# A gated recurrence and a routed feed-forward on one core: TensorE in program order, expert blocks over all turns, two weight buffers

## The chip, the cores and the metric

The kernel runs on one core of a Trainium2 chip. The core has a matrix engine (TensorE, PE in the profile; its weight loads are PEld), VectorE (DVE), ScalarE (ACT), GpSimd (POOL), and a sync engine (SP) that issues DMAs; GpSimd issues the indirect ones. Each engine works through its own queue in order and waits on semaphores for the others. The metric is the device time of one execution in microseconds; lower is better.

## The reference

Two parts, all in float32. First a recurrence over time, for 4 batches, 8 heads, 768 steps and head width 48:

```python
f = 1.0 / (1.0 + np.exp(-f_logit))
for t in range(S):
    state = f[:, :, t, :, None] * state + np.einsum('bhd,bhe->bhde', k[:, :, t], v[:, :, t])
    y[:, :, t] = np.einsum('bhd,bhde->bhe', q[:, :, t], state)
```

Then y, as 3072 rows of 384, goes through a feed-forward of 8 experts, two for each row:

```python
noisy_logits = x @ w_gate + np.log1p(np.exp(x @ w_noise)) * noise
top2 = np.argpartition(-noisy_logits, 2, axis=1)[:, :2]
# top2_w: softmax over the two chosen logits
for e in range(E):
    for k in range(2):
        mask = top2[:, k] == e
        h = np.maximum(x[mask] @ w1[e], 0.0)
        out[mask] += top2_w[mask, k, None] * (h @ w2[e])
```

w1 of an expert is 384 x 1024, w2 1024 x 384: 1.5 MB each.

## The kernel before

**The recurrence** is done in six chunks of 128 steps. `chunk(c, b)` handles one chunk of one batch, all eight heads. Inside a chunk the sum over earlier steps is built in seven levels (steps within pairs, fours, eights, up to 128), so that a chunk is a fixed list of matmuls: transposes of f, q and k (L208), the diagonal (`diag`, L231), for each level 16 score matmuls (`sc`, L247), then y from the scores A and v (L268) plus, from the second chunk on, y from the carried state (L272), and transposes and products for the next state (`kp` L281, `xp` L286, `ds` L295). Between two levels, the scores of the level are copied under a mask into A (copy_predicated on VectorE, L253), qP is multiplied by the decay T (VectorE, L257), and kQ and T are multiplied on GpSimd (L259, L261). The next level's `sc` reads qP and kQ, so a level cannot begin before these are done. The last chunk needs no next state and leaves out `kp` and `ds`.

**Routing.** `route(c)` follows the four batches of a chunk: logits (`lg`, L316), noise, the two best experts of each row, and a running place of each row in its expert's list (`rk`, L354, the last matmuls of the routing). Eight indirect DMAs from GpSimd then write row numbers into a table in DRAM, `ids` (L369, one for each batch and choice), and four DMAs write the rows with their gates to `xd` (L349). `choose(c)` picks from the filled lists LIST[c] blocks of 128 rows of one expert each (0, 9, 8, 8, 8 and 22: 55 in all), and writes where in `ids` each begins (`row_no`) and whether its weights must be loaded (`load_no`): the load is skipped if the block that used the same weight buffer last, NW blocks back, had the same expert.

**A block.** `fetch` issues the loads of a block, on SP: the block's row numbers from `ids` into `places` (L441), two weight loads into one of NW buffers each (L446), and on GpSimd the gather of rows from `xd` into `rows_in` (L447; three buffers). `block` then does: transposes (`bx`, L458), copy to `xT` (L460, VectorE), the gate weights (`gw` L466, VectorE), 24 matmuls by w1 in two halves (`bh`, L475) with a relu each (L479, ScalarE), an indirect read of the 128 output rows (L480, GpSimd), eight matmuls by w2 (`by`, L486), the sum (L489, VectorE) and an indirect write of the output rows (L490, GpSimd). `block` is a generator with seven yields.

**What sets the order.** The batches of a chunk run as two streams, batches 0 then 2 and 1 then 3; a pair of batches advances together, one level of each in a turn. `weave` takes one yield of each stream per turn and, in proportion to the turns done, yields of `filler`, the blocks of the earlier lists. That is the order in which the instructions are written. The order in which each engine issues them is set by a scheduler that places the instructions of all engines by its own estimates. On TensorE it put pair 1 of chunks 2 to 5 alone behind each routing (but for the first block's `bx`) and the blocks after it, some of them alone and the rest between the levels of pair 2. After `choose(c)` the next block is fetched at once (L550), then the rest of the earlier blocks is done, and in the last chunk two blocks are kept for after the routing. What is not woven is emitted after the last chunk: the tail, 24 blocks. PSUM has two buffers of two banks (scores and y) and four of one bank (the rest).

Of the kernel before, what the change touches and what calls it, by code (L numbers as in the profile page):

```python
# [8 lines left out]
F32 = mybir.dt.float32  # L9
# [4 lines left out]
ALU = mybir.AluOpType  # L14
# [6 lines left out]
def kernel(  # L21
# [31 lines left out]
    nc = tc.nc  # L53
    B, H, S, D = q.shape
# [4 lines left out]
    NCH = S // C  # L59
# [8 lines left out]
    XW = DM + E  # L68
    BIG = 1 << 20
    LIST = [0, 9, 8, 8, 8, 22]  # L70
    FIRST = [0, 0, 5, 0, 4, 0]
    NB = sum(LIST)
    NW = 3
    assert (H * D, 1 << NL, B * S, FO) == (DM, C, N, 8)
    assert all(sum(LIST[:c + 1]) <= max(0, 2 * B * (c + 1) - E + 1) for c in range(NCH - 1))
    assert NB == 2 * N // C + E - 1
# [4 lines left out]
    wk = ctx.enter_context(tc.tile_pool(name="wk", bufs=2))  # L81
# [25 lines left out]
    for l in range(NL - 1):  # L107
        m, nb = 1 << l, HC >> l
# [75 lines left out]
    xrow = [None] * NCH  # L184
# [12 lines left out]
    def chunk(c, b):  # L197
        u = f"_{c}_{b}"
        n = (c * B + b) % NLD
        last = c == NCH - 1  # L200
        vt = vts.pop((c, b))
        yTc = yT[c % 2]

        def transposed(nm):
            p = one_bank(f"{nm}p{u}")
            flat = pads[nm][n].rearrange("t h d -> t (h d)")
            for hp in range(HP):
                nc.tensor.transpose(p[:, hp * C:(hp + 1) * C], flat[:, hp * 128:(hp + 1) * 128], ident)  # L208
            return p

        fT = wk.tile([128, HP * C], F32, tag="T0", name=f"f{u}")
        nc.scalar.activation(fT, transposed("f"), AF.Sigmoid)
        qT = wk.tile([128, HP * C], F32, tag="qT", name=f"qT{u}")
        qpsum = transposed("q")
        nc.scalar.copy(qT, qpsum)
        qP = wk.tile([128, HP * C], F32, tag="qP", name=f"qP{u}")
        nc.vector.tensor_tensor(qP, qpsum, fT, ALU.mult)
        kQ = wk.tile([128, HP * C], F32, tag="kQ", name=f"kQ{u}")
        nc.scalar.copy(kQ, transposed("k"))

        def rows(par):
            return slice(par * DP, par * DP + D)

        def cols(hp):
            return slice(hp * C, (hp + 1) * C)

        A = wk.tile([C, 2, HP * C], F32, tag="A", name=f"A{u}")
        sc = two_banks(f"diag{u}")
        for hp in range(HP):
            for par in range(2):  # L230
                nc.tensor.matmul(sc[:, par, cols(hp)], lhsT=kQ[rows(par), cols(hp)], rhs=qT[rows(par), cols(hp)],  # L231
                                 start=True, stop=True)
        nc.vector.tensor_tensor(A.rearrange("j r (a i) -> j (r a) i", i=C), sc.rearrange("j r (a i) -> j (r a) i", i=C),
                                ident.unsqueeze(1).broadcast_to((C, H, C)), ALU.mult)
        yield

        T = fT
        for l in range(NL):
            m, nb = 1 << l, HC >> l
            x = HP * nb  # L240
            qv = qP.rearrange("d (x two m) -> d x two m", two=2, m=m)[:, :, 1, :]
            kv = kQ.rearrange("d (x two m) -> d x two m", two=2, m=m)[:, :, 0, :]
            nj = C if l < NL - 1 else HC
            sc = two_banks(f"sc{l}{u}")
            for hp in range(HP):
                for par in range(2):
                    nc.tensor.matmul(sc[0:nj, par, hp * HC:(hp + 1) * HC].rearrange("j (a m) -> j a m", m=m),  # L247
                                     lhsT=kQ[rows(par), hp * C:hp * C + nj],
                                     rhs=qv[rows(par), hp * nb:(hp + 1) * nb, :], start=True, stop=True)
            Av = A.rearrange("j r (x two m) -> j r x two m", two=2, m=m)[0:nj, :, :, 1, :]  # L250
            scv = sc[0:nj, :, 0:HP * HC].rearrange("j r (x m) -> j r x m", m=m)
            if l < NL - 1:
                nc.vector.copy_predicated(Av, masks[:, l].rearrange("j (r x m) -> j r x m", r=2, m=m), scv)  # L253
            else:
                nc.scalar.copy(Av, scv)  # L255
            Tv = T.rearrange("d (x two) -> d x two", two=2)
            nc.vector.tensor_tensor(qv, qv, Tv[:, :, 0:1].broadcast_to((128, x, m)), ALU.mult)  # L257
            if l < NL - 1 or not last:
                nc.gpsimd.tensor_tensor(kv, kv, Tv[:, :, 1:2].broadcast_to((128, x, m)), ALU.mult)  # L259
                Tn = wk.tile([128, x], F32, tag=f"T{l + 1}", name=f"T{l + 1}{u}")  # L260
                nc.gpsimd.tensor_tensor(Tn, Tv[:, :, 0], Tv[:, :, 1], ALU.mult)  # L261
                T = Tn
            yield

        y = two_banks(f"y{u}")
        for hp in range(HP):
            for par in range(2):
                nc.tensor.matmul(y[rows(par), par, cols(hp)], lhsT=vt[:, 2 * hp + par, :], rhs=A[:, par, cols(hp)],  # L268
                                 start=True, stop=(c == 0))
            if c:  # L270
                for par in range(2):
                    nc.tensor.matmul(y[rows(par), par, cols(hp)], lhsT=state[b][rows(par), hp, :],  # L272
                                     rhs=qP[rows(par), cols(hp)], start=False, stop=True)
        for par, copy in ((0, nc.scalar.copy), (1, nc.vector.tensor_copy)):
            copy(yTc[rows(par), :, b, :], y[rows(par), par, :].rearrange("e (a t) -> e a t", t=C))
        yield

        if not last:
            kp = one_bank(f"kp{u}")
            for hp in range(HP):  # L280
                nc.tensor.transpose(kp[:, hp * 128:(hp + 1) * 128], kQ[:, cols(hp)], ident)  # L281
            kn = wk.tile([C, H * DP], F32, tag="kn", name=f"kn{u}")
            nc.scalar.copy(kn, kp)
        xp = one_bank(f"xp{u}")
        for hp in range(HP):
            nc.tensor.transpose(xp[:, hp * 128:(hp + 1) * 128], yTc[:, hp, b, :], ident)  # L286
        nc.scalar.copy(xrow[c][:, b, 0:DM].rearrange("t (h d) -> t h d", d=D),
                       xp.rearrange("t (h d) -> t h d", d=DP)[:, :, 0:D])
        if last:
            return  # L290
        ds = one_bank(f"ds{u}")
        for hp in range(HP):
            for par in range(2):
                h = 2 * hp + par
                nc.tensor.matmul(ds[par * DP:(par + 1) * DP, hp * D:(hp + 1) * D], lhsT=kn[:, h * DP:(h + 1) * DP],  # L295
                                 rhs=vt[:, h, :], start=True, stop=True)
        dsv = ds[:, 0:HP * D].rearrange("d (a e) -> d a e", e=D)
        new = wk.tile([128, HP, D], F32, tag=f"st{b}", name=f"st{u}")
        if c == 0:
            nc.vector.tensor_copy(new, dsv)  # L300
        else:
            nc.vector.tensor_tensor(new, state[b], T.unsqueeze(2).broadcast_to((128, HP, D)), ALU.mult)
            nc.vector.tensor_tensor(new, new, dsv, ALU.add)
        state[b] = new
        yield
# [187 lines left out]
        yield  # L493

    YIELDS = 7
    AHEAD = 2
    queue = [(c, i) for c in range(NCH) for i in range(LIST[c])]
    fetched = [0]

    def fetch_to(n):  # L500
        while fetched[0] < n:
            fetch(*queue[fetched[0]])
            fetched[0] += 1

    def blocks(lo, hi, ready):
        for g in range(lo, hi):
            fetch_to(min(g + 1 + AHEAD, ready))
            yield from block(*queue[g])


# [10 lines left out]
            yield from chunk(c, b)  # L521
            load_to(c * B + b + 1 + NLD)

    def weave(c, filler, n):

        turns, done, t = 2 * (NL + 3 - (c == NCH - 1)), 0, 0
        streams = [chunks(c, range(0, B, 2)), chunks(c, range(1, B, 2))]
        while streams:
            for x in list(streams):
                if next(x, streams) is streams:  # L530
                    streams.remove(x)
            t += 1
            while done < min(n, n * t // turns):
                next(filler, None)
                done += 1

    load_to(NLD)
    load_router()
    clear()
    done = 0  # L540
    for c in range(NCH):
        xrow[c] = wk.tile([128, B, XW], F32, tag="xrow", name=f"xrow{c}")
        ready = sum(LIST[:c])
        keep = 2 if c == NCH - 1 else 0
        filler = blocks(done, ready, ready)
        weave(c, filler, YIELDS * (ready - done - keep))
        route(c)
        if LIST[c]:
            choose(c)
            fetch_to(ready + min(1, LIST[c]))  # L550
        for _ in filler:
            pass
        done = ready
    for _ in blocks(done, NB, NB):
        pass


# [26 lines left out]
```

## Time and profile before

| | |
|---|---|
| runs, median of 3 | 1343.76 us (1341.33 to 1353.79) |
| profiled execution | 1334.09 us, span 1332.4 us, mean granted TensorE clock 0.845 |
| `bh` matmuls, L475 | 340.0 us busy |
| `by` matmuls, L486 | 293.8 us busy |
| `sc` matmuls, L247 | 241.4 us busy |
| weight loads (L446) | 110 DMAs of 1536 KB, 9.1 us from issue to landing (median), some of them skipped |
| gathers (L447) | 55, 6.1 us to landing (median) |
| id scatters (L369) | 48, 3.8 us to landing (median) |

The page gives busy time per engine, the span in 40 slices of 33.3 us (a digit is the busy share in tenths; PEclk is the clock granted to TensorE, in tenths of full), the DMA queues, the groups of instructions with their mean durations and the idle time ahead of them, and the DMAs with their time to landing. The trace adds lists of waits, a timeline by engine and tables for any stretch.

The `rk` matmuls of the six routings start at 123.6, 238.40, 440.32, 633.75, 828.55 and 991.90 us; they divide the span into stages. The stage that ends with the routing of chunk c is called chunk c below, and what follows the last one the tail. The stages of chunks 2 to 5 last 201.9, 193.4, 194.8 and 163.3 us, the tail 340.5. Blocks done in them: 9, 8, 8, 6 and 24.

### The profile page before, as it was taken

To read this page: it belongs to the slowest core of one execution; us is meant where nothing else is said; L and a number is where in the kernel's file an instruction comes from. 1 tells how busy PE (TensorE), PEld (TensorE's weight loads), DVE (VectorE), ACT (ScalarE), POOL (GpSimd) and SP (SyncE) were. 2 spreads that over 40 slices of the span, in tenths; PEclk is the share of its full clock that TensorE was granted. 3 is DMA by queue.
4 is the path that set the end of the run, shared out by engine and by line. 5 is a ranking of instruction groups with operands and counts; after the bars stand their busy time and mean duration, and the time that the engine had idled before them with its cause. 6 is when DMAs were issued, how large, how long until landed. Compare 5 with 4: busy or idle time off the path is not lost. (4 is left out here: it accounts for less than half of the span.)

```text
span 1332.4 us, 21528 instructions
## 1 busy us (share of the span) xinstructions
PE 1119.6 (84%) x8461; PEld 905.7 (68%) x8461; DVE 399.5 (30%) x1046; ACT 189.0 (14%) x322; POOL 428.4 (32%) x602
## 2 busy tenths in 40 slices
PE   4597799599999599998699998799985788888887
PEld 3586667577787567786577786767764676766675
DVE  3354543631331530341621442613430011001010
ACT  1024021210201201212110213011020010000010
POOL 9732521432331332331432331514312122222221
PEclk9976565659999659999659998679878799999999
DMA  8732130367871358841367831188331978677710
GB/s 108 294 48 53 21 48 13 61 256 282 260 241 31 67 185 298 300 149 31 60 258 282 264 129 48 28 328 317 127 140 23 356 291 295 248 278 260 285 53 1
DMA packets 199748, 227.01 MB, mean 170 GB/s; under 512 B 115280, under 2 KB 171763, under 8 KB 198624
## 3 DMA queue, kind: packets, MB, share of 16 engines
q1 hardware_dynamic: 186096, 187.32, 43.8%
q0 software_dynamic: 13552, 38.33, 8.5%
q8 instruction: 67, 1.10, 0.4%
q14 instruction: 33, 0.27, 0.1%
HBM read 213.89 MB, written 25.30 MB: 180 GB/s over the span
## 5 line engine op out<-in xcount | busy, mean ns | idle before, releaser
L475 PE MATMUL bh<-xT,w 128*128 128x128 f32 x2640 | 340.0, 291 | 47.8 <-DVE xT L460 47.1
L475 PEld LDWEIGHTS bh<-xT,w 128*128 128x128 f32 x2640 | 324.7, 204 | 61.5 <-DVE xT L460 56.3
L247 PE MATMUL sc<-qP,kQ 48*128 48x64 f32 (+1 forms) x2688 | 241.4, 354 | 82.1 <-POOL kQ L259 58.6
L247 PEld LDWEIGHTS sc<-qP,kQ 48*128 48x128 f32 (+1 forms) x2688 | 228.2, 263 | 97.4 <-POOL kQ L259 64.0
L486 PE MATMUL by<-w,h 128*128 128x384 f32 x880 | 293.8, 487 | 0.0
L486 PEld LDWEIGHTS by<-w,h 128*128 128x128 f32 x880 | 162.9, 190 | 102.2
L490 POOL DMA_INDIRECT out_dram<-rows_out,places x55 | 56.1, 1021 | 391.6 <-DVE rows_out L489 333.8
L253 DVE COPY_PREDICATED A<-masks,sc 128x512 f32<-128x512 uint8 x144 | 130.2, 904 | 128.4 <-PE sc L247 101.2
L479 ACT ACTIVATE h<-bh 128x512 f32<-128x512 f32 x110 | 65.7, 597 | 628.6 <-PE bh L475 628.6
L259 POOL TENSOR_TENSOR kQ<-kQ,T 128x256 f32<-128x256 f32 x140 | 95.5, 687 | 92.6 <-PE sc L247 91.3
L466 DVE TENSOR_TENSOR gw<-picks,rows_in 128x8 f32<-128x8 f32 (+2 forms) x71 | 10.5, 166 | 377.0 <-DMA rows_in<-xd,places 377.0
L369 POOL DMA_INDIRECT ids<-tokens,ati x48 | 48.1, 1003 | 165.4 <-DVE have L393 70.5
L489 DVE SCALAR_TENSOR_TENSOR rows_out<-by,gt,rows_out 128x384 f32<-128x384 f32 x55 | 33.9, 616 | 197.7 <-PE by L486 182.4
L480 POOL DMA_INDIRECT rows_out<-out_dram,places x55 | 56.7, 1031 | 111.6 <-DMA out_dram<-rows_out,places 107.1
L447 POOL DMA_INDIRECT rows_in<-xd,places x55 | 56.2, 1022 | 92.2 <-DMA places<-ids 64.5
L257 DVE TENSOR_TENSOR qP<-qP,T 128x256 f32<-128x256 f32 x144 | 75.3, 523 | 19.4 <-PE sc L247 17.2
L255 ACT COPY A<-sc 64x512 f32<-64x512 f32 x24 | 13.6, 579 | 282.7 <-DVE qP L257 265.7
L268 PE MATMUL y<-A,v 128*48 128x128 f32 x384 | 52.2, 379 | 0.0
L458 PE MATMUL bx<-ident,rows_in 128*128 128x128 f32 x165 | 29.9, 293 | 24.8 <-DMA rows_in<-xd,places 24.2
L458 PEld LDWEIGHTS bx<-ident,rows_in 128*128 128x128 f32 x165 | 21.4, 150 | 41.4 <-issue 31.0
L272 PE MATMUL y<-qP,st 48*48 48x128 f32 x320 | 48.1, 374 | 0.0
L261 POOL TENSOR_TENSOR T<-T 128x128 f32<-128x128 f32 (+4 forms) x140 | 36.4, 263 | 9.5
(135 smaller groups left out, 744.4 us busy)
## 6 DMA issues: line engine op xcount, KB each, us to landing
w<-in_moe_w_dram SPq DMA_DIRECT2D x110, 1536.0 KB, 9.1
xd<-zero POOLq DMA_DIRECT2D x4, 1176.0 KB, 16.2
xd<-xrow SPq DMA_DIRECT2D x24, 196.0 KB, 2.2
f<-in_f_logit_dram SPq DMA_DIRECT2D x24, 192.0 KB, 4.2
q<-in_q_dram SPq DMA_DIRECT2D x24, 192.0 KB, 5.0
k<-in_k_dram SPq DMA_DIRECT2D x24, 192.0 KB, 4.9
v<-in_v_dram SPq DMA_DIRECT2D x24, 192.0 KB, 2.9
out_dram<-zero POOLq DMA_DIRECT2D x4, 1152.0 KB, 7.5
```

The lines of the kernel that those rows point to most:

```text
L247: nc.tensor.matmul(sc[0:nj, par, hp * HC:(hp + 1) * HC].rearrange("j (a m) -> j a m", m=m), lhsT=kQ[rows(par), hp * C:hp * C + nj], rhs=qv ...
L253: nc.vector.copy_predicated(Av, masks[:, l].rearrange("j (r x m) -> j r x m", r=2, m=m), scv)
L257: nc.vector.tensor_tensor(qv, qv, Tv[:, :, 0:1].broadcast_to((128, x, m)), ALU.mult)
L259: nc.gpsimd.tensor_tensor(kv, kv, Tv[:, :, 1:2].broadcast_to((128, x, m)), ALU.mult)
L268: nc.tensor.matmul(y[rows(par), par, cols(hp)], lhsT=vt[:, 2 * hp + par, :], rhs=A[:, par, cols(hp)], start=True, stop=(c == 0))
L447: nc.gpsimd.indirect_dma_start(out=xr, out_offset=None, in_=xd, in_offset=bass.IndirectOffsetOnAxis(ap=pl.bitcast(U32), axis=0), bounds_ch ...
L458: nc.tensor.transpose(xp[:, j * 128:(j + 1) * 128], xr[:, j * 128:(j + 1) * 128], ident)
L475: nc.tensor.matmul(hp[:, f * 128:(f + 1) * 128], lhsT=w1[:, j, fo * 128:(fo + 1) * 128], rhs=xT[:, j * 128:(j + 1) * 128], start=(j == 0), ...
L479: nc.scalar.activation(h[:, half * 4:half * 4 + 4, :].rearrange("p f t -> p (f t)"), hp, AF.Relu)
L480: nc.gpsimd.indirect_dma_start(out=yo, out_offset=None, in_=out, in_offset=bass.IndirectOffsetOnAxis(ap=pl, axis=0), bounds_check=N - 1, o ...
L486: nc.tensor.matmul(yp[:, 0:DM], lhsT=h[:, fo, :], rhs=w2[:, fo, :], start=(fo == 0), stop=(fo == FO - 1))
L490: nc.gpsimd.indirect_dma_start(out=out, out_offset=bass.IndirectOffsetOnAxis(ap=pl, axis=0), in_=yo, in_offset=None, bounds_check=N - 1, o ...
```

## The change

TensorE's instructions are no longer placed by the scheduler: the loop over the chunks is inside `tc.manual_schedule` for TensorE, so TensorE issues in the order in which the code is written. The other engines are still placed by the scheduler. One generator runs through all 55 blocks. `weave` spreads a chunk's blocks over all turns of both pairs (in chunk 2, the first with blocks, over the turns after the sixth); every chunk leaves three blocks of its list undone (KEEP), which are woven into the next chunk, so chunks 2 to 5 do 6, 8, 8 and 8 blocks and the tail 25. Blocks are fetched one ahead instead of two, and the fetch right after `choose` is gone: the next fetch is written at the start of the first kept block. There are two buffers for each weight instead of three. The multiply of qP is written before copy_predicated.

In the issue order of TensorE, the 20 turns of a chunk each have two or three quarter-steps of a block between the levels. In the chunks 0 and 1, without blocks, it differs in that the diagonal of a stream's batch comes before the transposes of the other stream's batch instead of among them. GpSimd's placed order still has the eight scatters of a routing among the T and kQ products of the next pair 1: in chunk 3 the two kQ products of level 0 stand behind the fifth and the sixth scatter, and those of level 1 behind the eighth.

```diff
-    NW = 3
+    NW = 2
...
+            Tv = T.rearrange("d (x two) -> d x two", two=2)
+            nc.vector.tensor_tensor(qv, qv, Tv[:, :, 0:1].broadcast_to((128, x, m)), ALU.mult)
             if l < NL - 1:
                 nc.vector.copy_predicated(Av, masks[:, l].rearrange("j (r x m) -> j r x m", r=2, m=m), scv)
             else:
                 nc.scalar.copy(Av, scv)
-            Tv = T.rearrange("d (x two) -> d x two", two=2)
-            nc.vector.tensor_tensor(qv, qv, Tv[:, :, 0:1].broadcast_to((128, x, m)), ALU.mult)
...
-    AHEAD = 2
+    AHEAD = 1
+    KEEP = 3
...
-    def blocks(lo, hi, ready):
-        for g in range(lo, hi):
-            fetch_to(min(g + 1 + AHEAD, ready))
+    ready = [0]
+
+    def blocks():
+        for g in range(NB):
+            fetch_to(min(g + 1 + AHEAD, ready[0]))
             yield from block(*queue[g])
...
-    def weave(c, filler, n):
+    def weave(c, filler, n, first):
...
-            while done < min(n, n * t // turns):
+            while done < min(n, n * (t - first) // (turns - first)):
                 next(filler, None)
                 done += 1
...
+    filler = blocks()
     done = 0
-    for c in range(NCH):
-        xrow[c] = wk.tile([128, B, XW], F32, tag="xrow", name=f"xrow{c}")
-        ready = sum(LIST[:c])
-        keep = 2 if c == NCH - 1 else 0
-        filler = blocks(done, ready, ready)
-        weave(c, filler, YIELDS * (ready - done - keep))
-        route(c)
-        if LIST[c]:
-            choose(c)
-            fetch_to(ready + min(1, LIST[c]))
+    with tc.manual_schedule(engines={mybir.EngineType.PE}):
+        for c in range(NCH):
+            xrow[c] = wk.tile([128, B, XW], F32, tag="xrow", name=f"xrow{c}")
+            n = max(0, ready[0] - done - KEEP)
+            weave(c, filler, YIELDS * n, 6 if done == 0 else 0)
+            done += n
+            route(c)
+            if LIST[c]:
+                choose(c)
+                ready[0] += LIST[c]
         for _ in filler:
             pass
-        done = ready
-    for _ in blocks(done, NB, NB):
-        pass
```

## The prediction

> **What bounds the kernel now.** The page first: TensorE is busy for 84% of the span and no other engine for more than 32%, so the question is when TensorE idles and at which clock it works.
>
> ```profile
> PE 1119.6 (84%) x8461; PEld 905.7 (68%) x8461; DVE 399.5 (30%) x1046; ACT 189.0 (14%) x322; POOL 428.4 (32%) x602
> PEclk9976565659999659999659998679878799999999
> ```
>
> Each digit is a slice of 33.3 us. PEclk is 5 or 6 in slices 4 to 9, 14 and 15, 20 and 21, and 26, and 9 for the most part between. The windows by stage (columns: window, its length, busy time of PE, PEld, DVE, ACT, POOL, granted clock, DMA share, GB/s) say what those slices are:
>
> ```profile
> 239.00:290.00 51.00, 41.65 (x350) 33.43 (x349) 28.13 (x79) 6.26 (x10) 25.30 (x39) 0.57 0.46 130
> 344.00:440.00 96.00, 87.87 (x759) 70.06 (x757) 31.74 (x73) 17.77 (x31) 27.64 (x41) 0.98 0.50 155
> 440.00:495.00 55.00, 42.35 (x351) 34.07 (x351) 28.90 (x86) 6.23 (x10) 24.90 (x39) 0.56 0.43 115
> 548.00:633.00 85.00, 77.18 (x696) 61.74 (x694) 31.50 (x69) 16.65 (x29) 25.73 (x39) 0.98 0.43 132
> ```
>
> After each routing the first pair of batches runs its recurrence alone, some 52 us at a clock of 0.56; later the second pair shares TensorE with expert blocks at 0.98. The timeline (start, duration, what ran, in brackets the idle time ahead and its releaser) prices the same 32 matmuls, a level of both streams, in both surroundings:
>
> ```profile
> 464.35 3.68 PE L247 MATMUL sc<-qP,kQ 48*128 48x64 f32 x32 [1.12 <-POOL kQ L259]
> 586.90 2.00 PE L247 MATMUL sc<-qP,kQ 48*128 48x64 f32 x32
> ```
>
> 3.68 us against 2.00. A pair of batches takes about 26.1 us dense (transposes 2.6 and diagonal 2.2, six levels at 1.94 from start to start, the last 1.08, y 5.67, kp/xp/ds 2.95 and about 1.5 between). So 54 us at 440 to 495, less 26, is 28 us lost, in each of chunks 3, 4 and 5.
>
> Last, the end of the last routing, on GpSimd and then on TensorE:
>
> ```profile
> 1021.91 0.99 POOL L369 DMA_INDIRECT ids<-tokens,ati  x1 [2.50 <-DMA ids<-tokens,ati]
> 1025.91 0.97 POOL L369 DMA_INDIRECT ids<-tokens,ati  x1 [3.01 <-DMA ids<-tokens,ati]
> 1032.03 1.05 POOL L447 DMA_INDIRECT rows_in<-xd,places  x1 [5.14 <-DMA places<-ids]
> ...
> 1038.66 0.87 PE L458 MATMUL bx<-ident,rows_in 128*128 128x128 f32 x3 [19.65 <-DMA rows_in<-xd,places]
> 1040.18 8.48 PE L475 MATMUL bh<-xT,w 128*128 128x128 f32 x48 [0.65 <-DVE xT L460]
> ```
>
> The eight id scatters of a routing (L369) go one by one, each waiting for the one before to land: 995.72 to 1025.91 is 30.2 us for seven steps, 4.3 each. The first read of ids after them (L441), the gather (L447) and its landing add 12.75 us to bx. From rk, where the routing leaves TensorE (991.90), to the bx that needs its ids is 46.8 us; in chunk 2 it is 285.13 - 238.40 = 46.7.
>
> **The change part by part.**
>
> *Spreading the blocks.* All of the 28 us per chunk would come back if each turn of pair 1 always had a block to do. 30 woven blocks over 20 turns give 2.8 quarter-steps a turn, about 4.4 us of block beside 1.94 us of level; that is denser than 344 to 440, so I take clock and durations from there.
>
> *What the spread blocks wait for.* fetch reads ids, so it waits for all eight scatters of the routing written before it. With AHEAD at 1, block 6 is fetched before routing 2 is written and block 7 after it; likewise 14/15, 22/23 and 30/31. In the issue order TensorE does the transposes, block 6, levels 0 and 1, then bx of block 7. The scatters lie on GpSimd beside the T and kQ products as before, so bx(7) can go at rk + 47. Ahead of it TensorE has 11.04 us of block 6, the transposes and diagonals, and two levels; before, level 1 began 19.2 us after rk (459.55), its kQ products placed on GpSimd behind the fourth scatter; now they stand behind the fifth and the sixth, 4 to 8 us later. Level 1 and the by of block 6 take 7.1 us more: rk + 31 to 35, taken as 33. TensorE idles 14 us and, in program order, levels 2 to 6 wait with it. Before, pair 1 filled these 47 us. So most of the 28 us is paid again as a wait.
>
> Stage by stage, rk to rk. Chunks 3 and 4: 47 to bx; 2.8 us that the first bh takes longer after idling (8.48 at 1040.18, 5.62 dense); then seven blocks at 11.04 (bx .42, bh 5.46, by 5.16) = 77.3, levels 2 to 6 8.84, y 5.67, kp/xp/ds 2.95, pair 2 26.1, routing logits to rk 9.63 (5.99 of it idle), gaps 5.3: 135.8; 1.5 for the kQ products behind the scatters: 187.1. Before: 193.4 and 194.8. Gain 14.0 together.
>
> Chunk 5 has no kp and ds (4.1 less over both pairs) and so 183.0; before 163.3 with six blocks, now eight. Loss 19.7.
>
> Chunk 2 takes six blocks, not nine: 46.7 + 2.8 + rest of pair 1 10.2, pair 2 26.1, six blocks 66.2, xT waits 3.7, 9.63, gaps 3.0 = 168.3; before 201.9. Gain 33.6. Its first six turns get no block, so pair 1 stays at 0.57 there.
>
> Tail: block 30 is done 15 us after rk, then bx(31) waits to rk + 46.8. 24 blocks follow, where 22 took 287.5 us from 1038.66: 287.5 + 2 x 11.96 = 311.4. With fewer weight loads (below) I take 3 us off; with a drain of 6.3 this is 361.5; before 340.5. Loss 21.0.
>
> *Program order in chunks 0 and 1.* diag of the first batch now stands ahead of the second batch's transposes and waits for the copy of kQ: .73 us in the row at 448.05, some .6 a pair, four pairs: 2.4 lost.
>
> *qP ahead of copy_predicated.* Waits of sc on qP sum to 0.9 us in the profile, those on kQ to 58.6, so this is worth at most 0.9; taken as 0. It makes the reading of PSUM later by one multiply, 523 ns; the 4.4 us of block between two levels cover that, and without them (six turns of chunk 2, and chunks 0 and 1) it would cost up to .5 a level; there the kQ wait (1.12 at 464.35) ends later.
>
> *Two weight buffers.* Loads are skipped when the expert is that of the block NW back. From the inputs' routing I count 44 loads, not 52: 25 of 163 MB less, 15 loads for the last 22 blocks instead of 19. A buffer is free one block later: w1 of g+2 waits for bh of g, about 18 us before its use; a load lands in 9.1 us (median). Covered in the tail; without cover up to 9.1 a block. For blocks 7, 15, 23, 31 the weights are issued .84 us after the ids read (1029.15 and 1029.99), so land about when the rows do: 0 to 3 us each, taken as 0.
>
> Sum: 240.8 to rk of chunk 1 (238.4 + 2.4), 168.3, 187.1, 187.1, 183.0, 361.5: 1327.8 against 1332.4. The profiled execution took 1334.09, 1.7 beyond its span; the median of the runs, 1343.76, is 0.7% above it. (1327.8 + 1.7) x 1343.76 / 1334.09 = 1339.
>
> **A rule weighed.** The dense rows bear on one point more: bh at 1040.18, after 19.65 us idle, took 2.9 us longer than warm. The Trainium skill, "TensorE: Matmul & The Clock Gate", section "Why this matters for your kernels", advises against TensorE idling beyond about 3 us between bursts, as the clock then returns to half. That speaks against this change where it puts bx(7) in the way of the levels, and it agrees with this row. An estimate by the page's window of about 3.4 us to warm up: 1.7 us lost per stall instead of 2.8, four stalls, 4 us less in the sum.
>
> **The rivals.**
>
> *Shorter scatter chain, tidier tail (faster).* The scatters' fastest landing is 2.7 us, where 3.8 is the median; fewer weights in flight while they run could bring each step from 4.3 to 3.3: 7 us in each of four stages, 28. The tail lost 24.4 us over its 22 blocks beyond 11.96 each, to gathers landing in 6 us; eight loads fewer might give back half, 12. Together 40 less: about 1299. For it: DMA stands at a share of .27 in 992 to 1038. Against: the steps there are 4.3 already.
>
> *In-order stalls (slower).* DVE waits 377.0 us for gathered rows at gw (L466), 14.6 at the longest. Before, TensorE's placed order had other work there; in program order a level's qP or copy queued behind gw on DVE holds TensorE and all that follows. At 2 us for each of 30 woven blocks: 60 us, 1399. From 0.75 us a block (22 us) it decides for slower. For it: the tail's xT waits of 2 to 3 us in about every second block. Against: a woven block lasts about 17 us, a gather lands in 6.1.
>
> *The wait on ids does not matter (much faster).* If bx(7) were not held, chunks 3, 4 and 5 would give back 28 each and the tail some 20: about 1235. Nothing in the profile speaks for it: 46.7 and 46.8 us stand in two stages.
>
> **How the numbers follow.** The sum as worked out: 0.60, with its own range 1313 to 1363 (the stalls at 10 to 17 us instead of 14 in three chunks, weights 0 to 12, gaps 2 to 12 a chunk, not all at one end). Faster rival 0.15, ids wait absent 0.02, slower rival 0.23. About 1% (13 us) is what a measurement of this kernel tells from no change. Of the main case a third lies below 1330, four tenths within 1%, a quarter above 1357: faster .20 + .17 = .37; same .25; slower .15 + .23 = .38. The range reaches into both rivals: 1290 to 1385.
>
> **What would show it.** Right: rk of chunk 1 near 241 and stages near 168, 187, 187, 183; in each of chunks 3 to 5 a bx with some 14 us idle on the gather at rk + 47, and one of some 30 us after the last routing; the clock up only behind it. Wrong: no such idle (ids come early); many idle times of 1 to 3 us before sc on DVE (in-order stalls); bh or by waiting on DMA w (the two buffers); clock under 0.9 in the woven stretches.

## The result and the profile after

The changed kernel takes 1417.5 us in the median (1413.17 to 1425.57), the kernel before, run beside it, 1342.55. The ratio is 1.055, with a 95% interval of 1.047 to 1.063. The forecast was 1339 us in a range to 1385, so it is 5.9% off and on the wrong side. The profiled execution has a span of 1423.9 us; the forecast in that scale was 1327.8, so 96.1 us are to be found.

The page of the changed kernel, engines and granted clock by slices of 35.6 us:

```profile
PE 1111.5 (78%) x8461; PEld 905.8 (64%) x8461; DVE 397.1 (28%) x1046; ACT 188.7 (13%) x322; POOL 441.4 (31%) x602
PEclk7567565589978698987897888899868899998899
```

TensorE is busy for 8 us less and idle for 100 us more. The long troughs of the clock are gone from slice 10 on, but in their place stand many digits of 7 and 8: the clock goes up and down all the time. The woven stretches of chunks 3 and 4, from the `bx` that waits for the ids to the next rk, show it (the columns are those of the prediction's windows; the clock is the third number from the end):

```profile
473.00:631.00 158.00, 141.10 (x1165) 113.89 (x1165) 47.78 (x112) 24.51 (x43) 45.00 (x60) 0.89 0.54 166
680.00:842.00 162.00, 142.03 (x1165) 114.86 (x1165) 47.21 (x111) 24.51 (x43) 45.31 (x60) 0.87 0.47 143
```

The forecast had taken its durations from a stretch at 0.98.

By stages, from rk to rk, in us:

| stage | before | forecast | measured | off by |
|---|---|---|---|---|
| to rk of chunk 1 | 238.4 | 240.8 | 239.5 | -1.3 |
| chunk 2 | 201.9 | 168.3 | 183.6 | +15.3 |
| chunk 3 | 193.4 | 187.1 | 208.5 | +21.4 |
| chunk 4 | 194.8 | 187.1 | 210.7 | +23.6 |
| chunk 5 | 163.3 | 183.0 | 187.9 | +4.9 |
| tail | 340.5 | 361.5 | 393.7 | +32.2 |

The list of waits of the changed kernel (engine, line, releaser: us in total, times, longest):

```profile
PE bh L475 <- DVE xT L460: 98.7, 42, 7.2
PE bx L458 <- DMA rows_in<-xd,places: 75.9, 6, 30.1
POOL rows_out L480 <- DMA out_dram<-rows_out,places: 183.8, 48, 8.1
```

In the kernel before these were 47.1, 24.2 and 107.1. The first two lines grew by 103 us together, about as much as the 100 us more of idle time. The second line is the wait behind the id scatters that was forecast; TensorE's timeline shows it in chunk 3 and after the last routing:

```profile
473.05 0.90 PE L458 MATMUL bx<-ident,rows_in 128*128 128x128 f32 x3 [13.03 <-DMA rows_in<-xd,places]
...
1075.20 0.87 PE L458 MATMUL bx<-ident,rows_in 128*128 128x128 f32 x3 [30.14 <-DMA rows_in<-xd,places]
```

They stand 50.0 and 45.0 us after their rk. The growth of the first and the third line was not in the sum. A piece of the tail shows how they hang together; first GpSimd, then VectorE, then TensorE, in the same 20 us of the changed kernel:

```profile
1294.82 1.02 POOL L490 DMA_INDIRECT out_dram<-rows_out,places  x1 [7.57 <-DVE rows_out L489]
1302.37 1.02 POOL L480 DMA_INDIRECT rows_out<-out_dram,places  x1 [6.54 <-DMA out_dram<-rows_out,places]
1304.94 1.02 POOL L447 DMA_INDIRECT rows_in<-xd,places  x1 [1.55 <-DMA places<-ids]
```

```profile
1310.86 0.17 DVE L466 TENSOR_TENSOR gw<-picks,rows_in 128x8 f32<-128x8 f32 x1 [15.80 <-DMA rows_in<-xd,places]
1310.95 0.61 DVE L489 SCALAR_TENSOR_TENSOR rows_out<-by,gt,rows_out 128x384 f32<-128x384 f32 x1
1311.48 0.55 DVE L460 COPY xT<-bx 128x384 f32<-128x384 f32 x1
```

```profile
1305.68 0.49 PE L458 MATMUL bx<-ident,rows_in 128*128 128x128 f32 x3
1312.08 7.49 PE L475 MATMUL bh<-xT,w 128*128 128x128 f32 x48 [5.91 <-DVE xT L460]
```

The write of the output rows (L490) is issued at 1294.82 and lands 7.5 us later; only then can L480 go, and so can the read of ids for the next block, which overwrites the row numbers that the write was using; behind these comes the gather. The gather lands at about 1310.8. Its gw stands on VectorE ahead of L489 and xT of the block that TensorE is at, whose bx was done at 1306.2. So TensorE waits 5.91 us for a block that it does not need yet, and then runs the first part of bh at half clock: 7.49 us instead of 5.62.

What is new is the 7.5 us. The DMA summary of L490, minimum, median and maximum of us to landing, is for the kernel before and then for the changed one:

```profile
DMA to landing us min/median/max: 2.1/2.7/6.9
```

```profile
DMA to landing us min/median/max: 2.1/5.4/8.8
```

On SP's queue a weight load is issued at 1293.91, the moment by ends: with two buffers w2 of block g+2 takes the place of w2 of block g, which by of g has just finished reading. In the kernel before, SP's loads are issued elsewhere in the block (1206.32, 3.4 us after the write at 1202.89, which had landed by 1205.77, when the L480 that waited for it was issued).

The changed kernel's own trace holds the comparison, since loads of an expert that is already there are skipped. A skipped load takes SP 0.07 to 0.09 us to issue (22 of the 110; the other 88 take 0.37 us or more). First the real load of the piece above, then a skipped one at the same place, 0.9 us ahead of the write, with what follows on GpSimd:

```profile
1293.91 0.38 SPq L446 DMA_DIRECT2D w<-in_moe_w_dram  x1
```

```profile
717.27 0.07 SPq L446 DMA_DIRECT2D w<-in_moe_w_dram  x1
718.17 1.03 POOL L490 DMA_INDIRECT out_dram<-rows_out,places  x1 [3.97 <-DVE rows_out L489]
721.02 1.02 POOL L480 DMA_INDIRECT rows_out<-out_dram,places  x1 [1.81 <-DMA out_dram<-rows_out,places]
```

This L480 goes 2.85 us after its write was issued, not 7.55. Over all writes whose landing the trace holds (52 of 55): 29 with a real load issued at most 3 us ahead or 0.5 us behind land in 6.2 us (median, 4.5 to 8.8); 10 with a skipped load there in 2.6 (2.1 to 4.5); 13 with none there in 2.6 too (median).

In the woven stages the late write reaches TensorE by another way. In chunk 3 a write issued at 534.67 holds L480 until 541.04; then GpSimd, VectorE and TensorE go on like this:

```profile
541.04 1.07 POOL L480 DMA_INDIRECT rows_out<-out_dram,places  x1 [2.68 <-DMA out_dram<-rows_out,places]
542.83 1.94 POOL L261 TENSOR_TENSOR T<-T 128x128 f32<-128x128 f32 x6
544.80 0.36 DVE L302 TENSOR_TENSOR st<-st,T 128x192 f32<-128x192 f32 x1 [4.32 <-POOL T L261]
545.08 1.22 DVE L233 TENSOR_TENSOR A<-diag,ident 128x1024 f32<-128x1024 f32 x1
546.21 0.55 DVE L460 COPY xT<-bx 128x384 f32<-128x384 f32 x1
546.81 2.93 PE L475 MATMUL bh<-xT,w 128*128 128x128 f32 x12 [5.89 <-DVE xT L460]
```

T stands on GpSimd behind L480, the state product (`st`) and the diagonal's copy stand on VectorE behind T, and xT stands behind both.

### The profile page after: what moved, and what is told of

It reads as the page before. It is cut to its first block, busy times and chain, and to the rows that moved or that the text cites. A ratio compares the mean times of both kernels' runs of the same rounds, so it can differ in the third digit from the quotient of the medians.

```text
span 1423.9 us, 21431 instructions
## 1 busy us (share of the span) xinstructions
PE 1111.5 (78%) x8461; PEld 905.8 (64%) x8461; DVE 397.1 (28%) x1046; ACT 188.7 (13%) x322; POOL 441.4 (31%) x602
## 5 line engine op out<-in xcount | busy, mean ns | idle before, releaser
L475 PE MATMUL bh<-xT,w 128*128 128x128 f32 x2640 | 370.6, 307 | 99.3 <-DVE xT L460 98.7
L475 PEld LDWEIGHTS bh<-xT,w 128*128 128x128 f32 x2640 | 353.5, 219 | 114.3 <-DVE xT L460 109.1
L247 PE MATMUL sc<-qP,kQ 48*128 48x64 f32 (+1 forms) x2688 | 217.0, 329 | 63.1 <-POOL kQ L259 41.2
L247 PEld LDWEIGHTS sc<-qP,kQ 48*128 48x128 f32 (+1 forms) x2688 | 204.9, 240 | 79.7 <-POOL kQ L259 45.4
L490 POOL DMA_INDIRECT out_dram<-rows_out,places x55 | 56.7, 1031 | 344.5 <-DVE rows_out L489 282.8
L259 POOL TENSOR_TENSOR kQ<-kQ,T 128x256 f32<-128x256 f32 x140 | 104.9, 759 | 132.5 <-PE sc L247 131.3
L466 DVE TENSOR_TENSOR gw<-picks,rows_in 128x8 f32<-128x8 f32 (+2 forms) x71 | 11.7, 184 | 391.6 <-DMA rows_in<-xd,places 391.6
L253 DVE TENSOR_TENSOR qP<-qP,T 128x256 f32<-128x256 f32 x144 | 70.2, 489 | 171.3 <-PE sc L247 124.1
L480 POOL DMA_INDIRECT rows_out<-out_dram,places x55 | 57.1, 1039 | 189.5 <-DMA out_dram<-rows_out,places 183.8
L489 DVE SCALAR_TENSOR_TENSOR rows_out<-by,gt,rows_out 128x384 f32<-128x384 f32 x55 | 33.9, 616 | 164.4 <-PE by L486 149.5
L231 PE MATMUL diag<-qT,kQ 48*128 48x128 f32 x384 | 33.4, 323 | 21.6 <-ACT kQ L219 21.6
L268 PE MATMUL y<-A,v 128*48 128x128 f32 x384 | 46.4, 344 | 0.0
L231 PEld LDWEIGHTS diag<-qT,kQ 48*128 48x128 f32 x384 | 28.2, 221 | 28.4 <-ACT kQ L219 28.4
L460 DVE COPY xT<-bx 128x384 f32<-128x384 f32 x55 | 30.2, 549 | 38.6 <-PE bx L458 38.5
```

What stands on the lines that cost most here:

```text
L475: nc.tensor.matmul(hp[:, f * 128:(f + 1) * 128], lhsT=w1[:, j, fo * 128:(fo + 1) * 128], rhs=xT[:, j * 128:(j + 1) * 128], start=(j == 0), ...
L480: nc.gpsimd.indirect_dma_start(out=yo, out_offset=None, in_=out, in_offset=bass.IndirectOffsetOnAxis(ap=pl, axis=0), bounds_check=N - 1, o ...
L490: nc.gpsimd.indirect_dma_start(out=out, out_offset=bass.IndirectOffsetOnAxis(ap=pl, axis=0), in_=yo, in_offset=None, bounds_check=N - 1, o ...
```

## The experiments

Theories at the start: B, two buffers move the weight loads onto the output writes and make gathers late; D, VectorE's placed order hands that lateness to TensorE; P, program order on TensorE costs by itself. A ratio is to the kernel before, run on the same chip in the same batch. The stages are those of one profiled execution of each, which lies up to 0.8% from the median of its runs; stage differences of under some 10 us are weak for that reason.

| run | what | ratio, 95% interval | chunks 2 to 5, us | tail, us |
|---|---|---|---|---|
| before | | 1 | 753.5 | 340.5 |
| changed | | 1.055 (1.047 to 1.063) | 790.7 | 393.7 |
| a1 | changed, three buffers | 1.037 (1.031 to 1.044) | 792.0 | 366.9 |
| a2 | changed, VectorE in program order | 1.029 (1.023 to 1.036) | 780.7 | 357.1 |
| a3 | changed, TensorE placed | 1.028 (1.022 to 1.034) | 744.0 | 386.0 |
| a4 | changed, three buffers, two ahead | 1.021 (1.013 to 1.029) | 770.9 | 355.7 |
| c1 | a4 with VectorE in program order | 0.988 (0.985 to 0.992) | 729.5 | 340.4 |
| c3 | a4 with TensorE placed | 0.994 (0.990 to 0.998) | 733.3 | 354.9 |
| c4 | before, VectorE in program order in the tail | 0.994 (0.990 to 0.998) | 752.8 | 333.2 |
| d1 | c1, kept blocks fetched before the routing | 0.971 (0.967 to 0.974) | 726.7 | 339.6 |
| d2 | c1, copy_predicated first | 0.988 (0.985 to 0.992) | 739.0 | 334.6 |
| d3 | c1, one ahead | 1.021 (1.015 to 1.027) | 767.1 | 354.6 |
| d4 | c1, blocks in pair 2 alone | 1.020 (1.015 to 1.025) | 774.2 | 343.2 |
| e2 | before, one ahead | 1.015 (1.011 to 1.019) | not given | not given |
| e3 | before, TensorE in program order | 1.087 (1.080 to 1.093) | 867.6 | 345.4 |
| e4 | before, two buffers, one ahead | 1.054 (1.045 to 1.062) | 795.0 | 364.1 |

With the changed kernel's KEEP, chunks 2 to 5 do 30 blocks and the tail 25; with that of before (before, c4, e2, e3, e4) 31 and 24.

**a1, three buffers.**

```diff
-    NW = 2
+    NW = 3
```

> The changed kernel with three weight buffers again, nothing else undone. Theory B (two buffers): w2 of block g+2 cannot be issued before by of g has ended, so both loads, the write of the output rows and the next read of ids fall together, gathers land late and TensorE waits for xT (98.7 us against 47.1 before). Then the tail falls from 393.7 us to about 362 and the stages of chunks 3 to 5 by some 8 each: about 1360 us. Theory D (VectorE's placed order: gw of the next block, waiting for its gather, stands ahead of xT and of the level's multiplies): within 15 us of 1417, as the order of gw stays. Theory P (TensorE's program order by itself): within 15 us of 1417 too. The waits of bx for rows behind the scatters (10 to 13 us in chunks 3 to 5, 30 in the tail) stay by all three.

1394.49 us, 23 below the changed kernel: less than B's 1360, and more than D and P allow. The tail fell by 26.8 us, as theory B has it, and L490 lands in 2.7 us again (median of the 17 landings that this trace holds), with L480's waits back at 99.8 us. The woven stages did not move (792.0), and neither did their waits for xT (45.0 us, 43.5 in the changed kernel, 14.8 before). So two buffers cost the tail 27 us, and something else holds the weave.

**a2, VectorE in program order.**

```diff
-    with tc.manual_schedule(engines={mybir.EngineType.PE}):
+    with tc.manual_schedule(engines={mybir.EngineType.PE, mybir.EngineType.DVE}):
```

> The changed kernel with VectorE in program order as well, so that gw of a block follows xT of the same block. Theory D: the 98.7 us of bh waiting for xT fall below 40, the clock stays up with them, and the time falls by 50 to 80 us to about 1340 to 1365. Theory B: the gather itself is late, so the wait moves from xT to bx (rows_in) and less than 25 us are gained. Theory P: no gain from this, or a loss, as one more engine is held to the written order.

xT's waits fell from 98.7 to 52.7 us and the tail by 36.6, with the two buffers left in; the whole gained 2.6% of before, 36 us by the medians, less than the 50 expected of D and more than the 25 of B. Late gathers reach TensorE through gw on VectorE, at least in the tail. What a short wait costs shows here best, in chunk 3 on TensorE:

```profile
497.01 2.93 PE L475 MATMUL bh<-xT,w 128*128 128x128 f32 x12 [2.24 <-DVE xT L460]
499.87 3.68 PE L247 MATMUL sc<-qP,kQ 48*128 48x64 f32 x32
503.48 6.97 PE L475 MATMUL bh<-xT,w 128*128 128x128 f32 x36
...
522.81 4.29 PE L475 MATMUL bh<-xT,w 128*128 128x128 f32 x36
```

After 2.24 us of waiting, 13.6 us of work run that take 7.9 at full clock (1.60, 2.00 and 4.29). The wait costs 2.2 + 5.7 us.

**a3, TensorE placed.**

```diff
-    with tc.manual_schedule(engines={mybir.EngineType.PE}):
+    if True:
```

> The changed kernel with TensorE placed by the scheduler again; the spread blocks, KEEP 3, one ahead and two buffers stay as written. Theory P: back to 1345 or below. Theory B: the tail stays near 390 us and the time above 1390. Theory D: in between, as the order of VectorE is placed anew together with TensorE's; no number.

1379.19 us, in between: the tail stays near 390, as B has it, and the woven stages fall by 46.7 us, as P has it, with chunk 2 at 168.0. With two buffers and one ahead, the scheduler's order waits less than the written one. The edit lets VectorE's order be placed anew too, so the two are not parted.

**a4, three buffers and two ahead.**

```diff
-    NW = 2
+    NW = 3
...
-    AHEAD = 1
+    AHEAD = 2
```

> The changed kernel with three weight buffers and with blocks fetched two ahead, so that two of the three kept blocks are fetched before the routing and only the third waits for the eight scatters. By the dependence on ids, the 13.0, 10.7 and 12.8 us of idle time ahead of the second kept block's bx in chunks 3 to 5 go, and of the 30.1 us in the tail about 11 (one more block done meanwhile). Theory B: 45 us below the kernel with three buffers alone, about 1315. Theories D and P: the same 45 us below 1417, about 1370.

1371.56 us, 46 below the changed kernel: what D and P named (about 1370), and not B's 1315. But a1 had already taken 23 of the 46, which D and P did not allow, so no theory has both. The waits of bx fell to 28.8 us as expected, and the second half of the 45 us did not come: the waits for VectorE stayed (xT 77.6) or grew (A 30.5, 21.5 in the changed kernel).

**b1, two buffers in the kernel before.** NW = 2 alone. With two buffers, two ahead loads the weights of block g+2 over those of block g before g runs, so its blocks use other weights and wait for them.

> The kernel before with two weight buffers, nothing else changed. Theory B, as the three-buffer run left it (27 us of the tail): the tail grows from 340.5 us by 20 to 30, the stages before it by 0 to 10: some 1370 us. If two buffers cost only where TensorE is in program order: within 10 us of before.

1759.87 us, which says nothing on B: the edit makes each block wait for loads that belong to a later one. It does show that two buffers force one ahead: bh waits 391.6 us for weights.

**c1, all three.** The edits of a2 and a4 together.

> The changed kernel with three buffers, two ahead and VectorE in program order together. If these take away different waits: tail near 342 us, chunks 2 to 5 near 760 together (790.7 in the changed kernel, 753.4 before), in all about 1350, even with before. If they take away the same waits: no better than 1365. Theory P: chunks 2 to 5 stay above 755 whatever is done to the others, since the placed order of the same blocks took 743.9.

1313.57 us, 1.2% below before, and 36 us below what was expected. Undone singly in the changed kernel, a2 took 10 us off chunks 2 to 5 and a4 19.8; together they take 61.2. So the two edits are worth much more together than one by one; while one late path was left, TensorE seems to have waited for that one. And chunks 2 to 5 are below 755, so theory P as stated falls.

**c3, the same with TensorE placed.** The edit of a3 on a4.

> The changed kernel with TensorE placed by the scheduler, three buffers and two ahead: what is left of the change is the spread of the blocks over all turns, KEEP 3 and the order of the qP multiply. Theory P and B together: chunks 2 to 5 near 735 us, tail near 347: about 1336 us, the same as before within 1%. If the spread itself costs: above 1360.

0.994 (0.990 to 0.998), with chunks 2 to 5 at 733.3 us, near the 735 expected. Against a4, which differs in TensorE's order alone, that is 37.6 us less: with early fetches but VectorE placed, TensorE in program order is still dear. Against c1 it is 3.8 us more: with VectorE in program order too, the written order costs nothing that shows. Early fetches alone are not enough.

**c4, the tail of before.**

```diff
-    for _ in blocks(done, NB, NB):
-        pass
+    with tc.manual_schedule(engines={mybir.EngineType.DVE}):
+        for _ in blocks(done, NB, NB):
+            pass
```

> The kernel before with VectorE in program order in the tail alone (gw of a block after its xT). Theory D: the xT waits of 2 to 3 us in every second tail block and the half clock behind them go, 15 to 21 us of the tail's 340.5: about 1327 us. Theory B: the gathers stay late, so bx waits instead and less than 6 us are gained.

1327.24 us, 0.6% faster (0.2 to 1.0), and the tail 7.3 us shorter, not 15 to 21. Between the two, nearer to B's: the tail's waits for xT fell from 32.3 to 24.2 us and did not move to bx (21.1, now 21.9). D is real in the kernel before too, at under half of the size.

**d1, the kept blocks fetched before the routing.**

```diff
+            fetch_to(ready[0])
             route(c)
```

> The version with three buffers, two ahead and VectorE in program order, and all three kept blocks fetched before the routing is written. By the dependence on ids the third kept block no longer waits for the scatters: in the tail the 9.98 us ahead of its bx go or shrink to what the scatters still hold of the block behind it; 5 to 10 us less, about 1306. In chunks 3 to 5, where no bx waits any more, nothing is gained. If the time stays within 3 us of 1313.6, the routing's 45 us bind through the scatters on GpSimd (kQ and the read of output rows behind them) and not through the gather.

1296.79 us, 2.9% below before and the best of all, more than expected. Its wait moved rather than went: after the last routing, TensorE no longer waits for rows but, 8.18 us, for xT, behind an output read that stands behind the scatters on GpSimd (the second line; the 9.01 us in the first are xT behind the routing's own work on VectorE, and c1 has 9.0 there as well):

```profile
976.39 7.62 PE L475 MATMUL bh<-xT,w 128*128 128x128 f32 x48 [9.01 <-issue]
...
1009.64 8.06 PE L475 MATMUL bh<-xT,w 128*128 128x128 f32 x48 [8.18 <-DVE xT L460]
```

Its profiled execution (span 1305.2) is 0.8% above its median, so its stages cannot say where 17 us against c1 come from. That the gain is more than the 5 to 10 us expected is not explained.

**d2, copy_predicated first.** The qP multiply goes back behind copy_predicated in c1.

> The same version (three buffers, two ahead, VectorE in program order) with copy_predicated ahead of the qP multiply again, as in the kernel before. The prediction's value for this edit is 0, at most 0.9 us by the wait of sc on qP in the kernel before. Now that VectorE follows the written order and TensorE has block work between two levels, I expect within 5 us of 1313.6; if the qP multiply sets when a level can begin, 144 copies of 0.9 us stand ahead of it and the time grows by 20 us or more.

1318.14 us, ratio 0.988, the same as c1. In this version the edit is worth nothing that can be measured, as predicted.

**d3, one ahead in c1.**

```diff
-    AHEAD = 2
+    AHEAD = 1
```

> Three buffers and VectorE in program order, but one block ahead as in the changed kernel. It parts the distance ahead from the order on VectorE. By the dependence on ids, bx of the second kept block waits again, 8 to 13 us in each of chunks 3 to 5 with the half clock behind it, and 20 to 30 us in the tail: 50 to 60 us above 1313.6, about 1368. If the distance matters only through late gathers on VectorE's queue, which program order has taken away: less than 25 us above.

1361.7 us, 48 above c1: bx waits 64.0 us for rows, six times, against 18.6. The distance ahead is worth what the wait on ids says.

**d4, blocks in pair 2 alone.**

```diff
-            weave(c, filler, YIELDS * n, 6 if done == 0 else 0)
+            weave(c, filler, YIELDS * n, 10)
```

> The version with three buffers, two ahead and VectorE in program order, with the blocks of every chunk woven into the second pair of batches alone, from turn 11 on, so that pair 1 runs alone as in the kernel before. It prices the spread by itself. By the prediction's reading of the profile, pair 1 alone costs 28 us more than dense in each of chunks 3 to 5, and the spread brings that back except for what the routing's 47 us hold: 15 to 25 us more in each of the three, about 1370. If the routing holds the spread blocks up as long as pair 1 ran alone, the spread is worth nothing: within 10 us of 1313.6.

1360.63 us, 47 above c1; chunks 3 to 5 are 12.8, 8.0 and 26.8 us longer. The spread pays, when its fetches are early.

**e1 to e4, the change's parts on the kernel before.** e1 takes two buffers and one ahead:

```diff
-    NW = 3
+    NW = 2
...
-    AHEAD = 2
+    AHEAD = 1
```

> The kernel before with two weight buffers and one block ahead (two ahead overwrites, with two buffers, the weights of a block that is still to run). This is the change's thrift in buffers alone, with TensorE and VectorE placed as before. By the parts measured in the changed kernel (three buffers -23 us, two ahead a further -23), 35 to 55 us slower than before, most of it in the tail: about 1380. If late gathers matter only where TensorE follows the written order: within 15 us of before.

1425.16 us, ratio 1.068, but with a wait of 48.63 us in it: the fetch behind the last routing loads block 33's weights over those of block 31, which is then computed with them. e4 leaves that fetch until block 31 has run:

```diff
-            fetch_to(ready + min(1, LIST[c]))
+            fetch_to(ready + min(1, LIST[c]) if c < NCH - 1 else ready)
```

> The kernel before with two buffers and one ahead, and no fetch right after the last routing, so that no block's weights are overwritten before it runs (in the run before this one block 31 used those of block 33 and TensorE stood 48.63 us for them). By that run's other stages (chunks 2 to 5 796.5 us, 753.5 before) and its tail without that wait, 45 to 75 us slower than before, 1380 to 1410: then two buffers and one ahead are the larger part of the loss by themselves, with TensorE placed. If they cost only with program order, within 20 us of before.

1403.59 us, ratio 1.054: as much as the whole change, though parts need not add up. Chunks 2 to 5 are 41.5 us longer than before and the tail 23.6, with TensorE placed by the scheduler. The summary of L490 in e4:

```profile
DMA to landing us min/median/max: 2.6/6.3/7.4
```

(this trace holds 10 of the 55 landings), and L480 waits 184.6 us for it over the whole run, 107.1 before. One ahead with three buffers:

> The kernel before with one block ahead and its three buffers. By the same parts, 15 to 30 us slower than before, and 20 or more below the run with two buffers; if the buffers' number is nothing by itself, equal to that run.

1.5% (1.1 to 1.9) slower, some 20 us, near the lower end of what was expected. The bx behind the last routing waits 28.80 us instead of 19.65; where the rest is lost is not shown. From here to e4's 5.4% it is the third buffer, taken away, and the fetch that e4 puts off. Last, program order for TensorE on the kernel before, with its own spread from the first turn and no kept blocks:

> The kernel before with TensorE in program order up to the tail, its own spread of the blocks from the first turn, no blocks kept (two in the last chunk), three buffers, two ahead. If program order by itself costs little once the fetches are early, as 729.5 against 733.3 us for chunks 2 to 5 says: within 20 us of before. By the dependence on ids it costs most here: bx of the first block stands ahead of level 0 in turn 1 and waits until 47 us after rk, with all levels behind it, so that nearly the whole 47 us are idle in chunks 2 to 5: each 30 us or more longer than with KEEP 3, about 1430.

1448.89 us, 8.7% slower. The first bx of each list stands ahead of level 0:

```profile
282.68 0.87 PE L458 MATMUL bx<-ident,rows_in 128*128 128x128 f32 x3 [34.24 <-DMA rows_in<-xd,places]
```

It comes 46.8 us after rk, and chunks 3 to 5 are 35.1, 33.9 and 28.6 us longer than before. KEEP in the change answers this wait, in part.

## Why the prediction was wrong

Two steps failed, one in the woven stages (65 of the 96 us) and one in the tail (32).

**In the weave, "so I take clock and durations from there" failed.** The sum takes dense durations, at a clock of 0.98, and one cold start of 2.8 us a stage. TensorE's clock behind the waiting bx was 0.89, 0.87 and 0.93 in chunks 3 to 5. What breaks it up, by the rows of chunk 3, are waits of bh for xT with half clock behind them; these waits are 43.5 us in chunks 2 to 5, 14.8 before. A wait of 2.24 us costs 5.7 us on top (a2). For chunk 3 the rows give an estimate of the 21.4 us over the forecast: bx comes 3.0 us later than rk + 47; three waits for xT behind it, of 5.89, 1.15 and 1.15 us, had no term but a share of "gaps 5.3"; and the matmuls behind these waits and behind bx take some 9 us longer than at full clock beyond the 2.8 counted. That is about 20. The other stages were not taken apart in this way. What makes xT late there is the order on VectorE and GpSimd together with late transfers, as in the piece of chunk 3 above; a2 takes 10 us off the weave, three buffers nothing by themselves, both together 23.6 (d3).

**In the tail, "Two weight buffers" failed.** It asked whether a load has time to land and found 18 us for 9.1; no wait on a weight load stands in the changed kernel's list, so that much held, and so did the count of 44 blocks that load (88 real loads of 110). It did not ask what else is in flight at the new moment of issue. Two buffers tie w2 to the end of by, just where the output rows are written, and a write with a real load beside it lands in 6.2 us instead of 2.6 (the skipped loads show that it is the load). L480, the gathers and the kQ and T products queue behind it on GpSimd, and the read of ids waits on SP. Taken as 3 us gained in the tail, it cost 26.8 there: with three buffers the tail is 366.9 us (a1), near the 361.5 forecast. On the kernel before, two buffers with the one ahead that they force cost 5.4% (e4).

**One ahead** was priced only by the wait on ids. That part held: bx 50.0, 48.3, 44.6 and 45.0 us after rk (47, 47, 47 and 46.8 forecast), with 13.0, 10.7, 12.8 and 30.1 us idle (14, 14, 14 and 31.8).

**Half clock by the page.** The estimate worked out from the Trainium skill, "TensorE: Matmul & The Clock Gate" (1.7 us a start) is further off than the 2.8; the limit of some 3 us of idle that its section "Why this matters for your kernels" gives is too wide for this kernel, where 2.24 us sufficed.

**The slower rival named the right queue,** but not what it would hold nor where. Program order on VectorE, which puts gw behind xT, gains 36 us by the medians (a2); in the profiled executions the tail is 36.6 us shorter and the weave 10. The rival spoke of the levels' qP and copies in the weave; waits of sc on qP do not stand in the list, and what gw and the state products held was xT of the block at hand. Against it the prediction set that a gather lands in 6.1 us and a block lasts 17; the gather's start, not its flight (4.2 us, median), is what the change delays. That its price, 60 us on the woven blocks, is near the 65 by which chunks 2 to 5 missed the forecast is luck.

**What held.** Of the 84 us that pair 1 alone was said to lose in chunks 3 to 5, the spread brings back a part: with early fetches it is worth 47 us in all (d4). qP first is worth nothing in c1 (d2); its waits were 2.5 us in the kernel before, not 0.9, which is the larger shape alone. Chunk 2's 168 us were not met in the changed kernel (183.6); a3, which has 168.0, has TensorE placed, so that agreement is no proof. The 2.4 us for diag's order stays unresolved: rk of chunk 1 lies between 235.9 and 243.2 us over the runs of the table. In the sum, the parts of a dense pair add up to 27.6 us, not 26.1: the 1.5 us between them were left out, 6 us over four stages. **The faster rival** failed: with fewer loads the tail got longer, and id scatters land in 4.2 us (median, 300 to 1000 us; 3.8 in the kernel before), not faster.

**Undone one by one** from the changed kernel: three buffers 1.8 points of the ratio, VectorE's order 2.6, both 3.4 (d3); two ahead on top of both 3.3 more (c1); fetching the third kept block before the routing 1.8 (d1). What is left open is how far the state products and how far gw hold xT inside the weave, since program order on VectorE moved both, and why chunks 2 to 5 of d3 (767.1) still stand 41.6 us over the forecast.

## What to carry to other kernels

Before a buffer is taken away, ask at which moment its load will now be issued and what small transfer lands at that moment, not only whether the load still has time. An engine put into program order hands every lateness of the others straight on, so first make the fetches early enough and write the other in-order engine's queue so that no early reader of late data stands ahead of the work that the first engine waits for; written order on TensorE cost the woven stages 47 us (a3) and 38 (a4 against c3) while VectorE's order was placed, and nothing that shows with early fetches and VectorE in written order too (c1 against c3). And price a wait on TensorE with the half clock behind it.

## What was unexpected of the hardware

A wait of little over 2 us was enough for half clock. In a2 bh waits 2.24 us, behind three transposes (bx), until 497.01, and the granted clock is 0.50 from 495.50 to 509.15 and 1.00 from there to 520. A wait of 1.15 us at 585.88 in the changed kernel slowed only the next 2.93 us (1.60 at full clock); the clock is 0.50 from 585.56 to 588.97.

Indirect writes of 128 rows land in 2.6 us (median) or, with a real weight load of 1.5 MB issued beside them, in 6.2; a load that is skipped at the same moment leaves 2.6.
